# A written-out order for the first of six token blocks: six weight loads issued together, its last second products ahead of block two, one operation moved from POOL to DVE

## The chip, the cores and the metric

The kernel runs on one core of a Trainium2 chip. The metric is the device time of one execution in microseconds (us). The core has engines that each work through their own queue of instructions in order: PE (matrix products, its weight loads are shown as PEld), DVE (elementwise work on vectors, scans, 32x32 transposes), ACT (activations, casts, copies), POOL (elementwise work, masks) and SP, which here only issues transfers (DMA). An instruction that waits holds up everything behind it on its engine.

## The reference, cut to what matters

```
def _attn_ref(q, k, v, alpha):                 # (4, 8, 768, 48): batch, heads, steps, head size
    for t in range(S):
        state = alpha[:, :, t, :, None] * state + einsum('bhd,bhe->bhde', k[:, :, t], v[:, :, t])
        y[:, :, t] = einsum('bhd,bhde->bhe', q[:, :, t], state)

x = attn_out as (3072 tokens, 384)
h = x @ w_in;  g = h * sigmoid(1.702 h);  x = g @ w_out        # layer 1: 384 -> 2048 -> 384
h = x @ w_in2; g = h - tanh(h);           out = g @ w_out2     # layer 2, same sizes
```

A decayed linear attention over 768 steps is followed by two two-matrix layers on 3072 tokens. Everything is float32; the weights reach the chip as pairs of 32-bit words that the kernel turns into float32.

## The kernel before, in words

**Tokens.** The 3072 tokens are 24 chunks of 128 steps (g = 0 to 23), and 6 blocks of 512 tokens. A layer's block needs four chunks of attention output: block one the chunks 0 to 3, block two 4 to 7, block three 8 to 11. Each layer goes through its 6 blocks, each block through 16 weight tiles m (128 of the 2048 hidden columns each): 96 steps s for layer 1, then 96 for layer 2.

**One step.** `gemm1` (L455, 9 products of 128x128 by 128x512) makes the hidden values of tile m in one of two banks, `sig_1` (ACT, L472) the activation, `g_hi` (ACT, L475) a rounded copy ghi, `g_lo` (DVE, L478) the remainder glo, and `gemm2` (L461, 9 products, the third of each three reads glo) adds the tile's share to the block's three output banks. Every float32 operand is split in two parts (hi and lo), hence 9 products for 3 slices. From block two on, `gemm2` of step s comes three steps behind `gemm1` (LAG). After the 16th `gemm2` `evac` copies the three output banks to `xs` (ACT L516 twice, DVE L513 once) and stores them.

**Weights of layer 1.** In block one each tile is loaded (`w_given`, 768 KB on SP's queue) and converted: `w_bits` (DVE, L172 and L173), `w_join` (DVE, L185), `w_hi` (ACT, L204), `w_lo` (DVE, L208). `gemm1` of tile m needs w_hi in its first product and w_lo in its third.

**Attention of a chunk.** `a_load` (four transfers), two scans of the decay (`a_scan`: DVE L257 to L259, and L261), `a_scale` (L265, L266: k and q times the decay), the scores (`s_mm` L296 with copies and a mask on POOL L310 for the chunks below 8; `a_whole` L325, masked on DVE L328, from chunk 8 = FULL on), `a_turn` (DVE L335, transposes of k, from chunk 8 on), `a_out` (PE: L351 the carried state, L358 the values, and in `a_delta` L372 the state's growth, which reads the transposes), `a_state` (DVE L381, L382), then out and back: `a_evac` copies y out (ACT L416) and writes it to DRAM (four transfers, L421), `a_back` reads it back in the layer's layout (L431), and `x_hi` (ACT L438), `x_lo` (DVE L442) split it.

**Order.** Until block six of layer 1 every engine keeps the order of the code. For block one that is a table of words, one word one call: g `gemm1`, s `sig_1`, i `g_hi`, f `g_lo`, u `gemm2`, w `w_given`, b `w_bits`, j `w_join`, H `w_hi`, L `w_lo` of a tile; a `a_load`, p and q the two scans, k `a_scale`, t `a_state`, d `a_guard`, S `s_mm`, c and y its copies, O `a_out`, E `a_evac` and `a_back` with the load of the chunk three further on, X `x_hi`, x `x_lo` of a chunk. So g15 is `gemm1` of tile 15, X7 the cast of chunk 7. These names are used below; numbers from 16 on are steps of block two (g16 is its first `gemm1`). From block two on, `steady` places the parts d = 0, 1, 2 and 5 of chunk c of the next block at the steps STARTS[c] + d. Part 0 has for chunk 8 alone its own first transposes, then for every chunk the first scan of the next chunk and `a_whole`; part 1 the second transposes, the next chunk's second scan and scaling; part 2 the next chunk's first transposes and `a_out`.

Of the kernel before, what the change touches and what calls it, by code (L numbers as in the profile page):

```python
# [68 lines left out]
def linear_attention_mlps(ctx, tc, xq, xv, fa, fv, cst, w1, w2, out):  # L69
    nc = tc.nc  # L70
    V, A, G, P, SP = nc.vector, nc.scalar, nc.gpsimd, nc.tensor, nc.sync
# [74 lines left out]
    bank = [ps.tile([128, 512], F32, name=f"bank{i}") for i in range(8)]  # L146
# [30 lines left out]
    def w_check(l, m):  # L177
        t = wt[m % 2]
        tc.keep_in_program_order(V.tensor_scalar(out=t, in0=w_high(raw[2 if l == 1 else m % 3]), scalar1=0x3800, scalar2=0x7800,  # L179
                                                 op0=ALU.bitwise_xor, op1=ALU.bitwise_and))  # L180
        A.activation(out=t.bitcast(BF16), in_=t, func=AF.Square, accum_out=wsum[:, (l - 1) * MT + m :][:, :1])  # L181
# [48 lines left out]
    def dec3(g, n):  # L230
        return pairs(dec(g, n))[:, :: 1 if n else -1]


    def qq(g):
        return dec3(g, 2)

    def qkk(g):
        return dec3(g, 3)
# [22 lines left out]
            V.tensor_tensor_scan(out=dec(g, 1), data0=dec(g, 1), data1=seg, initial=0.0, op0=ALU.mult, op1=ALU.max)  # L261

    def a_scale(g):
        e = V if g < FULL else G
        e.tensor_tensor(out=qkk(g), in0=qkk(g), in1=dec3(g, 0)[:, :, :C], op=ALU.mult)  # L265
        e.tensor_tensor(out=qq(g)[:, :, :C], in0=qq(g)[:, :, :C], in1=dec3(g, 1)[:, :, 1:], op=ALU.mult)  # L266

# [62 lines left out]
    def a_turn(g, low):  # L330
        k = pairs(place_of(g)[3])
        for x in (0, 2) if low else (1, 3):
            d = kt8[g % 2][:, 4 * D * (x // 2) + 32 * (x % 2) :][:, : NP * D].rearrange("p (a d) -> p a d", a=NP)[:, :, :32]
            for y in range(4):
                V.transpose(out=d[32 * y : 32 * y + 32], in_=k[32 * x : 32 * x + 32, :, 32 * y : 32 * y + 32])  # L335
# [39 lines left out]
    def a_state(g):  # L375
        c = g % NCH
        if c < NCH - 1:
            dl = bank[7][:DP, : NP * D].rearrange("p (a e) -> p a e", a=NP)
            al = dec3(g + 1, 0)[:, :, C:].to_broadcast([DP, NP, D])
            if c:  # L380
                V.tensor_tensor(out=state, in0=dl, in1=state, op=ALU.add)  # L381
                V.tensor_tensor(out=state, in0=state, in1=al, op=ALU.mult)  # L382
            else:
                V.tensor_tensor(out=state, in0=dl, in1=al, op=ALU.mult)
# [125 lines left out]
    def evac(l, t0, n, acc, ks=range(KT)):  # L510
        for k in ks:
            if k == 1:
                V.tensor_scalar(out=xs[:, k, :n], in0=acc[k][:, :n], scalar1=1 / 1.702 if l == 1 else 1.0, scalar2=None,  # L513
                                op0=ALU.mult)
            else:
                A.activation(out=xs[:, k, :n], in_=acc[k][:, :n], func=AF.Copy, scale=1 / 1.702 if l == 1 else 1.0)  # L516
            if l == 2:
                SP.dma_start(out=out[k, :, t0 : t0 + n], in_=xs[:, k, :n])
        if l == 1:
            SP.dma_start(out=x1t[:, :, t0 : t0 + n].rearrange("k p t -> p k t"), in_=xs[:, :, :n])  # L520
# [11 lines left out]
    LAG = 3  # L532
# [28 lines left out]
    def prep(g, part):  # L561
        if g >= NG:
            return
        if part < 2:
            a_scan(g, part)
        if part == 2:
            a_scale(g)
        if part == 3:
            a_guard(g)
# [11 lines left out]
        if r == 2:  # L581
            a_out(g, b)

    STARTS = (0, 3, 7, 10)

    def steady(g, d):
        if d == 0:
            if g == FULL:
                a_turn(g, 0)
            prep(g + 1, 0)  # L590
            a_whole(g, 5)
        if d == 1:
            a_turn(g, 1)
            prep(g + 1, 1)
            prep(g + 1, 2)
            prep(g, 3)
        if d == 2:
            if g + 1 < NG:
                a_turn(g + 1, 0)
            a_out(g, 5)  # L600
            a_state(g)
            a_done(g)
        if d == 5:
            x_hi(g)
            x_lo(g)
# [99 lines left out]
    NS, NS1 = len(steps), len(L1) * MT  # L705
# [8 lines left out]
    def pads():  # L714
        for t in (*late, spare):
            SP.dma_start(out=t[3][DP:], in_=xq[0, : 128 - DP, : NP * C])
# [23 lines left out]
        "X": lambda g: x_hi(g, bank[5] if g == 3 else None),  # L740
        "x": lambda g: x_lo(g, bank[5] if g == 3 else None),
        "z": lambda _: pads(),
    }
    for word in """
        X1 L1 X3 d3 a6 w8 w9 w10 x1 b2 j2 x3 g0 H2 b3 g1
        s0 i0 L2 j3 g2 s1 f0 H3 b4 i1 u0 s2 f1 i2 L3 j4
        g3 f2 H4 b5 u1 s3 i3 L4 j5 u2 b6 H5 L5 g4 j6 f3
        H6 g5 p4 s4 i4 t3 u3 s5 q4 i5 L6 g6 f4 f5 b7 u4
        s6 i6 k4 u5 d4 b8 j8 S40 f6 H8 u6 b9 c40 y40 j7 S41
        L8 H7 c41 L7 g7 y41 p5 q5 O4 s7 i7 k5 E4 w11 w12 g8  # L750
        t4 d5 f7 j9 S50 s8 p6 H9 u7 c50 L9 y50 i8 q6 S51 g9
        c51 k6 y51 f8 O5 s9 b10 X4 i9 j10 E5 z0 w13 w14 u8 t5
        H10 f9 d6 p7 S60 u9 c60 L10 y60 q7 S61 b11 g10 c61 y61 j11
        b12 H11 O6 s10 i10 L11 X5 j12 g11 E6 w15 f10 H12 k7 u10 s11
        i11 t6 d7 x4 L12 S70 g12 b14 c70 y70 f11 S71 b13 s12 i12 u11
        c71 j13 y71 X6 f12 H13 O7 x6 L13 x5 E7 j14 g13 b15 H14 u12
        s13 L14 i13 j15 f13 H15 g14 p8 L15 u13 s14 i14 q8 X7 f14 k8
        g15 x7 t7 u14 s15
    """.split():
        part[word[0]](int(word[1:]))  # L760

    for s in range(MT, NS + LAG):
        if s:
            if s <= NS:
                l, j, m, i, t0, n, acc = place(s - 1)
                prev = s - 1, n
        if s < NS:
            l, j, m, i, t0, n, acc = place(s)
            h = HB[s % 2][:, :n]
            gemm1(i, m, h, n)  # L770
            if l == 2:
                tanh_near(s, h)
        if s <= NS:
            g_split(*prev)
        if s < NS and l == 1:
            sig_1(s, h, n)
        if s == NS:
            u_flag()
        if s < NS:
            if l == 1 and j + 1 < len(L1):  # L780
                t1, n1 = L1[j + 1]
                for c in range(4):
                    steady(t1 // C + c, m - STARTS[c])
            if l == 1 and 0 < j < len(L1) - 1 and m - 2 in STARTS:
                w_check(1, 4 * (j - 1) + STARTS.index(m - 2))
            if l == 1 and 0 < j < len(L1) - 1 and m in STARTS:
                w_load(1, 4 * (j - 1) + STARTS.index(m), 2)
            if l == 2 and 2 <= j < 4:
                if m % 2:
                    w_check(l, 8 * (j - 2) + m // 2)  # L790
                else:
                    tc.keep_in_program_order(w_load(l, 8 * (j - 2) + m // 2))
            if l == 1 and j == len(L1) - 1:
                if m == 0:
                    for q in range(3):
                        w_load(2, q)
                if m == 1:
                    a_flag()
                if m == 4:
                    x1_load(0)  # L800
                if m in (6, 7, 8):
                    x1_split(0, m - 6)
                if m > 0:
                    conv(2, m >= 4)
            if l == 2:
                if cv[2] < 2 * MT:
                    conv(2)
                if j == 4 and m == 3:
                    w_flag()
                if j + 1 < len(L2):  # L810
                    if m == 3:
                        x1_load(j + 1)
                    if m in (6, 7, 8):
                        x1_split(j + 1, m - 6)
        if s >= LAG:
            l, j, m, i, t0, n, acc = place(s - LAG)
            if s >= NS or s - LAG < 15:
                continue
            gemm2(m, s - LAG, acc, n)
            if m == MT - 1:  # L820
                evac(l, t0, n, acc)
        if s == (len(L1) - 1) * MT - 1:
            in_order(begin)


    l, j, m, i, t0, n, acc = place(NS - 1)
# [118 lines left out]
```

## Time and profile before

| | |
|---|---|
| time, median of 3 runs (range) | 925.53 us (924.96 to 928.22) |
| the profiled execution, its own time | 924.23 us |
| its span in the profile | 922.5 us |
| PE busy | 905.8 us (98%) |
| DVE / ACT / POOL busy | 668.6 (72%) / 449.5 (49%) / 98.5 us (11%) |
| mean granted TensorE clock | 0.998 |

The span runs from the first to the last instruction; 1.7 us of the execution's time lie around it. Times in rows are us from the span's start. Products are pipelined: one 128x512 product lasts some 0.4 us from start to end, but the next one starts 0.23 us after it, so a group is measured from its first start to the next group's first start. A row's brackets give the idle time of the engine just before it, and what ended that.

### The profile page before, as it was taken

To read this page: it belongs to the slowest core of one execution; us is meant where nothing else is said; L and a number is where in the kernel's file an instruction comes from. 1 tells how busy PE (TensorE), PEld (TensorE's weight loads), DVE (VectorE), ACT (ScalarE), POOL (GpSimd) and SP (SyncE) were. 2 spreads that over 40 slices of the span, in tenths; PEclk is the share of its full clock that TensorE was granted. 3 is DMA by queue.
4 is the path that set the end of the run, shared out by engine and by line. 5 is a ranking of instruction groups with operands and counts; after the bars stand their busy time and mean duration, and the time that the engine had idled before them with its cause. 6 is when DMAs were issued, how large, how long until landed. Compare 5 with 4: busy or idle time off the path is not lost.

```text
span 922.5 us, 13368 instructions
## 1 busy us (share of the span) xinstructions
PE 905.8 (98%) x4941; PEld 716.2 (78%) x4941; DVE 668.6 (72%) x1129; ACT 449.5 (49%) x907; POOL 98.5 (11%) x82
## 2 busy tenths in 40 slices
PE   9899899999999999999999999999999999999996
PEld 5777677777777778777888888888888888888885
DVE  8999787747657585776499966767777777666663
ACT  5646533434433433434445645554655665545552
POOL 6112021101111110111001002002001001000000
PEclk9999999999999999999999999999999999999999
DMA  8856734324341532536253300201323310000001
GB/s 223 282 182 185 212 93 160 93 89 133 115 147 47 169 99 82 180 102 223 85 176 131 137 1 2 101 1 31 140 92 114 137 68 1 35 1 1 34 1 39
DMA packets 56315, 95.61 MB, mean 104 GB/s; under 512 B 4864, under 2 KB 35712, under 8 KB 56240
## 3 DMA queue, kind: packets, MB, share of 16 engines
q1 hardware_dynamic: 55952, 94.27, 32.1%
q8 instruction: 40, 0.66, 0.3%
q10 hardware_dynamic: 288, 0.40, 0.1%
q14 instruction: 35, 0.29, 0.1%
HBM read 80.88 MB, written 13.76 MB: 103 GB/s over the span
## 4 chain that ended last, share of the span: by engine, by line
PE 86%; DVE 8%; DMA 3%; issue 1%; ACT 1%; SPq 0%; DVEq 0%; ACTq 0%
PE bank L461 41%; PE bank L455 39%; DMA given<-w 2%; PE bank L358 2%; PE bank L325 2%; PE bank L619 1%; DVE glo L478 1%; PE bank L351 1%; DVE cf L173 1%; DVE cf L335 1%; DVE w L208 1%; DVE arena L261 1%; PE bank L372 1%; DVE arena L258 1%; DVE cf L185 1%
## 5 line engine op out<-in xcount | busy, mean ns | idle before, releaser
L455 PE MATMUL bank<-xhi,w 128*128 128x512 f32 x1152 | 392.3, 395 | 2.4 <-DVE w L208 1.7
L461 PE MATMUL bank<-ghi,w 128*128 128x512 f32 x1152 | 366.4, 398 | 1.1 <-ACT xs L516 1.1
L455 PEld LDWEIGHTS bank<-xhi,w 128*128 128x128 f32 x1152 | 216.0, 188 | 55.6 <-DVE w L208 2.7
L461 PEld LDWEIGHTS bank<-ghi,w 128*128 128x128 f32 x1152 | 213.7, 188 | 53.9 <-issue 1.5
L478 DVE TENSOR_TENSOR glo<-gt,ghi 128x512 fp32r<-128x512 f32 x192 | 136.3, 710 | 148.0 <-ACT ghi L475 145.9
L461 PE MATMUL bank<-glo,w 128*128 128x512 f32 x576 | 228.2, 396 | 2.1 <-DVE glo L478 2.1
L455 PE MATMUL bank<-xlo,w 128*128 128x512 f32 x576 | 227.5, 396 | 2.1 <-DVE xlo L442 2.1
L475 ACT CAST ghi<-gt 128x512 fp32r<-128x512 f32 x192 | 118.9, 619 | 204.0 <-DVE gt L492 130.2
L461 PEld LDWEIGHTS bank<-glo,w 128*128 128x128 f32 x576 | 108.2, 188 | 29.3 <-DVE glo L478 2.9
L455 PEld LDWEIGHTS bank<-xlo,w 128*128 128x128 f32 x576 | 108.2, 188 | 28.5 <-DVE xlo L442 2.5
L472 ACT ACTIVATE gt<-bank 128x512 f32<-128x512 f32 x96 | 57.3, 597 | 116.2 <-PE bank L455 112.2
L490 DVE SCALAR_TENSOR_TENSOR arena<-arena,bank 128x512 f32<-128x512 f32 x96 | 65.8, 685 | 31.1 <-ACT arena L488 30.0
L492 DVE SCALAR_TENSOR_TENSOR gt<-arena 128x512 f32<-128x512 f32 x96 | 68.3, 712 | 10.5 <-DVE arena L491 0.9
L488 ACT ACTIVATE arena<-bank 128x512 f32<-128x512 f32 x96 | 57.3, 596 | 38.3 <-PE bank L455 37.8
L489 ACT ACTIVATE arena<-arena,cs 128x512 f32<-128x512 f32 x96 | 69.6, 726 | 3.0
L491 DVE SCALAR_TENSOR_TENSOR arena<-arena 128x512 f32<-128x512 f32 x96 | 67.9, 707 | 3.1
L529 POOL TENSOR_TENSOR xlo<-arena,xhi 128x512 fp32r<-128x512 f32 x18 | 28.0, 1582 | 339.9 <-ACT xhi L528 339.9
L335 DVE STREAM_TRANSPOSE cf<-arena 32x128 f32<-32x128 f32 x176 | 53.2, 302 | 2.5
L181 ACT ACTIVATE wtb<-wtb 128x768 bf16<-128x768 int16 x32 | 26.8, 837 | 47.7 <-DVE wtb L179 47.7
L442 DVE TENSOR_TENSOR xlo<-xlo,xhi 128x384 fp32r<-128x384 f32 x22 | 14.5, 660 | 26.0 <-ACT xhi L438 26.0
L265 POOL TENSOR_TENSOR arena<-arena 112x512 f32<-112x512 f32 x11 | 14.0, 1272 | 118.0 <-DVE seg L259 86.9
L310 POOL TENSOR_SCALAR_AFFINE_SELECT arena<-arena 128x512 f32<-128x512 f32 x16 | 18.4, 1161 | 70.7 <-ACT arena L308 62.8
(137 smaller groups left out, 646.2 us busy)
## 6 DMA issues: line engine op xcount, KB each, us to landing
raw<-w SPq DMA_DIRECT2D x48, 768.0 KB, 4.4
given<-w SPq DMA_DIRECT2D x16, 768.0 KB, 8.3
arena<-xq SPq DMA_DIRECT2D x32, 224.0 KB, 4.9
x1t<-xs SPq DMA_DIRECT2D x6, 768.0 KB, 5.3
arena<-x1t SPq DMA_DIRECT2D x6, 768.0 KB, 4.7
out<-xs SPq DMA_DIRECT2D x17, 256.0 KB, 2.3
xlo<-xt SPq DMA_DIRECT2D x22, 192.0 KB, 2.6
xt<-arena SPq DMA_DIRECT2D x76, 48.0 KB, 1.7
```

Of the source, the lines that this page charges most:

```text
L335: V.transpose(out=d[32 * y : 32 * y + 32], in_=k[32 * x : 32 * x + 32, :, 32 * y : 32 * y + 32])
L455: P.matmul(out=h, lhsT=w[m][:, ws], rhs=x[:, k, :n], start=c == 0, stop=c == 3 * KT - 1)
L461: P.matmul(out=acc[k][:, :n], lhsT=w[m][:, ws], rhs=x[s % 3][:, :n], start=m == 0 and c == 0, stop=m == MT - 1 and c == 2)
L472: A.activation(out=gb(s)[:, :n], in_=h, func=AF.Silu, scale=1.702)
L475: A.copy(ghi[s % 3][:, :n], gb(s)[:, :n])
L478: V.tensor_tensor(out=glo[s % 3][:, :n], in0=gb(s)[:, :n], in1=ghi[s % 3][:, :n].bitcast(F32), op=ALU.subtract)
L488: A.activation(out=u, in_=h, func=AF.Square, accum_out=usum[:, s - NS1 :][:, :1])
L489: A.activation(out=w, in_=u, func=AF.Square, bias=pbias)
L490: V.scalar_tensor_tensor(out=p, in0=u, scalar=P3, in1=h, op0=ALU.mult, op1=ALU.mult)
L491: V.scalar_tensor_tensor(out=p, in0=u, scalar=-PR, in1=p, op0=ALU.add, op1=ALU.mult)
L492: V.scalar_tensor_tensor(out=gb(s), in0=w, scalar=PD, in1=p, op0=ALU.add, op1=ALU.mult)
L529: G.tensor_tensor(out=xlo[i][:, k], in0=xr[:, k], in1=xhi[i][:, k].bitcast(F32), op=ALU.subtract)
```

## The change

Block one has a new table. Six loads (w8 to w13) are issued together where three were; the other two follow after the first chunk's E. `gemm2` of tile n comes right behind `gemm1` of tile n+1 in most places; the last one (u15) and the block's `evac` (new word e) stand at the table's end, ahead of block two, where u15 and `evac` came in block two's third step. In block two `steady` starts its first two chunks (8 and 9) at steps 1 and 4 where it was 0 and 3, and the weight checks go with them. `a_scale` of chunk 8 runs on DVE where it was POOL.

```
     def a_scale(g):
-        e = V if g < FULL else G
+        e = V if g <= FULL else G
...
-    STARTS = (0, 3, 7, 10)
+    def starts(j):
+        return (0, 3, 7, 10) if j > 1 else (1, 4, 7, 10)
...
+        "e": lambda _: evac(1, 0, NB, bank[:3]),
     }
     for word in """
-        X1 L1 X3 d3 a6 w8 w9 w10 x1 b2 j2 x3 g0 H2 b3 g1
...
-        s13 L14 i13 j15 f13 H15 g14 p8 L15 u13 s14 i14 q8 X7 f14 k8
-        g15 x7 t7 u14 s15
+        X1 L1 X3 x1 d3 a6 w8 w9 w10 w11 w12 w13 x3 g0 b2 g1
...
+        f13 g14 j15 E7 x5 H15 x6 u13 s14 L15 i14 f14 p8 q8 g15 u14
+        s15 i15 f15 t7 u15 X7 x7 k8 e0
     """.split():
...
-        if s <= NS:
+        if MT < s <= NS:
             g_split(*prev)
...
-                    steady(t1 // C + c, m - STARTS[c])
-            if l == 1 and 0 < j < len(L1) - 1 and m - 2 in STARTS:
-                w_check(1, 4 * (j - 1) + STARTS.index(m - 2))
-            if l == 1 and 0 < j < len(L1) - 1 and m in STARTS:
-                w_load(1, 4 * (j - 1) + STARTS.index(m), 2)
+                    steady(t1 // C + c, m - starts(j)[c])
+            if l == 1 and 0 < j < len(L1) - 1 and m - 2 in starts(j):
+                w_check(1, 4 * (j - 1) + starts(j).index(m - 2))
+            if l == 1 and 0 < j < len(L1) - 1 and m in starts(j):
+                w_load(1, 4 * (j - 1) + starts(j).index(m), 2)
...
-            if s >= NS or s - LAG < 15:
+            if s >= NS or s - LAG < MT:
                 continue
```

**Place one.** DVE at the start of block one, before (w_456 is converted tile 1, given_65 the loaded tile 2, bank_110 holds chunk 3's values in the layer's layout):

```order
L208 TENSOR_TENSOR w_456<-cf_83,w_456 128x768
L442 TENSOR_TENSOR xlo_87<-xlo_87,xhi_85 128x3x128
L172 TENSOR_SCALAR cf_84<-given_65 128x768
L173 SCALAR_TENSOR_TENSOR cf_84<-given_65,cf_84 128x768
L185 SCALAR_TENSOR_TENSOR cf_84<-given_65,cf_84 128x768
L442 TENSOR_TENSOR xlo_87<-bank_110,xhi_85 128x3x128
```

The same place of the changed kernel:

```order
L208 TENSOR_TENSOR w_456<-cf_83,w_456 128x768
L442 TENSOR_TENSOR xlo_87<-xlo_87,xhi_85 128x3x128
L442 TENSOR_TENSOR xlo_87<-bank_110,xhi_85 128x3x128
L172 TENSOR_SCALAR cf_84<-given_65 128x768
L173 SCALAR_TENSOR_TENSOR cf_84<-given_65,cf_84 128x768
L185 SCALAR_TENSOR_TENSOR cf_84<-given_65,cf_84 128x768
L478 TENSOR_TENSOR glo_93<-gt,ghi_90 128x512
```

x3, which g0's seventh product reads, stood behind b2 and j2 and now stands ahead of them.

**Place two.** SP's queue from w8 (given_71) on, before; xt is the chunk's output in DRAM, xlo its read-back, arena the inputs of a later chunk:

```order
L162 DMA given_71<-w 128x1536
L162 DMA given_72<-w 128x1536
L162 DMA given_73<-w 128x1536
L421 DMA xt<-arena 48x2x128 x4
L431 DMA xlo_88<-xt 128x3x128
L251 DMA arena<-xq 112x516
L251 DMA arena<-xq 112x512
L251 DMA arena<-xq 112x4x128
L251 DMA arena<-xv 128x384
L162 DMA given_74<-w 128x1536
L162 DMA given_75<-w 128x1536
L421 DMA xt<-wtb 48x2x128 x4
```

And in the changed kernel:

```order
L162 DMA given_71<-w 128x1536
L162 DMA given_72<-w 128x1536
L162 DMA given_73<-w 128x1536
L162 DMA given_74<-w 128x1536
L162 DMA given_75<-w 128x1536
L162 DMA given_76<-w 128x1536
L421 DMA xt<-arena 48x2x128 x4
L431 DMA xlo_88<-xt 128x3x128
```

The loads of tiles 11 to 13 moved ahead of chunk 4's round trip (E4); those of 14 and 15 follow E4 in the changed kernel, where 13 and 14 followed E5 and 15 followed E6.

**Place three.** DVE at the border of blocks one and two, before, from f15 (glo_93) to the second transposes of chunk 8:

```order
L478 TENSOR_TENSOR glo_93<-gt,ghi_90 128x512
L335 STREAM_TRANSPOSE cf_82<-arena 32x4x32 x8
L257 MEMSET seg 112x4
L258 SCALAR_TENSOR_TENSOR raw<-raw,seg 112x516
L259 RECIPROCAL seg<-raw 112x4
L328 TENSOR_TENSOR arena<-bank_110,cs 128x512
L328 TENSOR_TENSOR arena<-bank_111,cs 128x512
L478 TENSOR_TENSOR glo_94<-gt,ghi_91 128x512
L335 STREAM_TRANSPOSE cf_82<-arena 32x4x32 x8
```

In the changed kernel, from chunk 8's scaling on:

```order
L265 TENSOR_TENSOR arena<-arena 112x512
L266 TENSOR_TENSOR arena<-arena 112x4x128
L513 TENSOR_SCALAR xs<-bank_106 128x512
L478 TENSOR_TENSOR glo_94<-gt,ghi_91 128x512
L335 STREAM_TRANSPOSE cf_82<-arena 32x4x32 x8
L257 MEMSET seg 112x4
L258 SCALAR_TENSOR_TENSOR raw<-raw,seg 112x516
L259 RECIPROCAL seg<-raw 112x4
L328 TENSOR_TENSOR arena<-bank_110,cs 128x512
L328 TENSOR_TENSOR arena<-bank_111,cs 128x512
L478 TENSOR_TENSOR glo_95<-gt,ghi_92 128x512
L335 STREAM_TRANSPOSE cf_82<-arena 32x4x32 x8
```

The transposes of chunk 8 now stand one glo further back: the first set behind f16 (glo_94), the second behind f17. On PE, chunk 8's `a_whole` now follows g17 and its `a_out` follows g19, where they followed g16 and g18; u15 stood behind that `a_out`, and u16 stands behind it now.

## Rows read from the trace of the kernel before

**Rows 1.** Stretches: length; busy PE, PEld, DVE, ACT, POOL (x instructions); clock; DMA share; GB/s.
```profile
32.04:120.25 88.21, 82.20 (x504) 61.91 (x504) 80.42 (x112) 47.43 (x100) 13.64 (x10) 1.00 0.69 214
...
136.69:915.00 778.31, 778.31 (x3996) 623.08 (x3996) 543.85 (x930) 375.33 (x733) 65.74 (x46) 1.00 0.27 88
```

**Rows 2.** Timeline of PE: start, us, instructions, and in brackets idle before.
```profile
35.78 0.96 PE L455 MATMUL bank<-xlo,w 128*128 128x512 f32 x3 [2.10 <-DVE xlo L442]
...
101.43 0.50 PE L461 MATMUL bank<-glo,w 128*128 128x512 f32 x1 [2.06 <-DVE glo L478]
...
111.96 0.73 PE L455 MATMUL bank<-xhi,w 128*128 128x512 f32 x2 [1.68 <-DVE w L208]
...
117.87 0.63 PE L461 MATMUL bank<-ghi,w 128*128 128x512 f32 x2
...
136.69 0.73 PE L461 MATMUL bank<-ghi,w 128*128 128x512 f32 x2 [1.06 <-ACT xs L516]
```

**Rows 3.** Timeline of DVE: the two long waits for loaded weight tiles.
```profile
98.78 0.56 DVE L172 TENSOR_SCALAR xs<-given 128x768 int32<-128x768 int32 x1 [3.72 <-DMA given<-w]
...
109.48 0.56 DVE L172 TENSOR_SCALAR cf<-given 128x768 int32<-128x768 int32 x1 [2.38 <-DMA given<-w]
```

**Rows 4.** The chain that ended last: one group of nine products, start and us.
```profile
141.13 2.09 PE bank L461 x9
```

**Rows 5.** Timeline of ACT: the cast i15, whose gemm1 ended where rows 2 have 117.87.
```profile
118.70 0.62 ACT L475 CAST ghi<-gt 128x512 fp32r<-128x512 f32 x1
```

**Rows 6.** Timeline of DVE: what the words L, j, f and b take.
```profile
37.10 0.95 DVE L208 TENSOR_TENSOR w<-cf,w 128x768 fp32r<-128x768 f32 x1
37.98 0.95 DVE L185 SCALAR_TENSOR_TENSOR xs<-given,xs 128x768 int32<-128x768 int32 x1
38.84 0.68 DVE L478 TENSOR_TENSOR glo<-gt,ghi 128x512 fp32r<-128x512 f32 x1
39.45 0.55 DVE L172 TENSOR_SCALAR xs<-given 128x768 int32<-128x768 int32 x1
40.03 0.96 DVE L173 SCALAR_TENSOR_TENSOR xs<-given,xs 128x768 int32<-128x768 int32 x1
```

**Rows 7.** Timeline of DVE: from f15 to chunk 8's second transposes.
```profile
120.50 0.69 DVE L478 TENSOR_TENSOR glo<-gt,ghi 128x512 fp32r<-128x512 f32 x1
...
123.79 0.06 DVE L257 MEMSET seg<- 112x4 f32 x1
...
125.25 1.26 DVE L328 TENSOR_TENSOR arena<-bank,cs 128x512 f32<-128x512 f32 x2
...
127.03 2.52 DVE L335 STREAM_TRANSPOSE cf<-arena 32x128 f32<-32x128 f32 x8
```

**Rows 8.** Timeline of PE: a_whole and a_out of chunk 8, and chunk 9's L372.
```profile
122.44 1.16 PE L325 MATMUL bank<-arena 48*128 48x128 f32 x16
...
127.91 0.66 PE L351 MATMUL bank<-arena,state 48*48 48x128 f32 x16
...
129.41 0.75 PE L372 MATMUL bank<-arena,cf 128*48 128x48 f32 x16
...
146.74 0.53 PE L372 MATMUL bank<-raw,cf 128*48 128x48 f32 x16
```

**Rows 9.** A stretch of block one, columns as in rows 1.
```profile
32.00:59.00 27.00, 24.86 (x106) 19.91 (x107) 26.14 (x39) 13.59 (x22) 0.00 (x0) 1.00 1.03 325
```

**Rows 10.** Timeline of SP's issues: the round trips of chunks 6 and 8.
```profile
92.41 2.69 SPq L421 DMA_DIRECT2D xt<-arena  x4
99.59 0.40 SPq L431 DMA_DIRECT2D xlo<-xt  x1
...
129.81 1.78 SPq L421 DMA_DIRECT2D xt<-arena  x4
...
133.10 0.40 SPq L431 DMA_DIRECT2D xlo<-xt  x1
```

**Rows 11.** Timeline of ACT: chunk 6's cast after that read-back.
```profile
102.19 0.51 ACT L438 CAST xhi<-xlo 128x384 fp32r<-128x384 f32 x1 [2.17 <-DMA xlo<-xt]
```

More of the change, by code (lines that the diff above doesn't have):

```diff
@@ L742, in linear_attention_mlps @@
         "z": lambda _: pads(),
+        "e": lambda _: evac(1, 0, NB, bank[:3]),
     }
     for word in """
-        X1 L1 X3 d3 a6 w8 w9 w10 x1 b2 j2 x3 g0 H2 b3 g1
[L746 to L756, printed above, removed]
-        s13 L14 i13 j15 f13 H15 g14 p8 L15 u13 s14 i14 q8 X7 f14 k8
-        g15 x7 t7 u14 s15
+        X1 L1 X3 x1 d3 a6 w8 w9 w10 w11 w12 w13 x3 g0 b2 g1
+        s0 j2 i0 H2 f0 b3 u0 s1 i1 L2 g2 j3 f1 H3 b4 u1
+        s2 i2 L3 f2 g3 j4 p4 H4 u2 s3 i3 L4 f3 g4 b5 j5
+        u3 s4 b6 H5 i4 L5 g5 f4 j6 b7 H6 u4 s5 i5 L6 g6
+        j7 f5 H7 q4 u5 s6 i6 k4 S40 t3 d4 L7 g7 f6 c40 p5
+        y40 S41 s7 q5 i7 u6 c41 k5 y41 O4 b8 j8 E4 w14 w15 S50
+        t4 H8 f7 d5 u7 L8 c50 b9 y50 S51 j9 g8 c51 b10 H9 y51
+        j10 O5 s8 i8 L9 H10 f8 X4 g9 L10 E5 z0 x4 p6 g10 s9
+        i9 q6 u8 s10 f9 i10 k6 u9 f10 t5 d6 b11 S60 X5 j11 u10
+        c60 b12 y60 H11 S61 L11 g11 c61 j12 y61 p7 H12 O6 s11 L12 i11
+        f11 E6 q7 g12 k7 u11 s12 b13 i12 f12 S70 j13 u12 c70 b14 y70
+        H13 L13 S71 g13 j14 c71 y71 t6 X6 H14 b15 O7 s13 i13 L14 d7
+        f13 g14 j15 E7 x5 H15 x6 u13 s14 L15 i14 f14 p8 q8 g15 u14
+        s15 i15 f15 t7 u15 X7 x7 k8 e0
     """.split():
```

## The prediction

> **What bounds the kernel now.** I read the stretches first. From 136.69 to 915 PE is busy in all 778.31 us [rows 1]: nothing there waits, and nothing there can give back or swallow what happens earlier. So whatever PE gains or loses before 136.69 reaches the end one to one. In block one and its border PE does wait: from 32.04, where g0 begins, to 120.25, where g16 begins, it is busy 82.20 of 88.21 us [rows 1], 6.01 idle. The timeline of PE names most of it: 2.10 us in g0 for x3, 2.06 for a glo, 1.68 for a w_lo [rows 2], the missing 0.17 in scraps. In block two it waits once more, 1.06 us at u16, for the block's evac on ACT [rows 2]. The timeline of DVE tells why a glo and a w_lo were late: DVE stood 3.72 and 2.38 us in front of b14 and b15, whose weight tiles had not landed [rows 3]. A seventh wait hides inside a group: L372 of chunk 8 took 0.75 us where that of chunk 9 took 0.53 [rows 8], because chunk 8's second transposes ended only at 127.03 + 2.52 = 129.55 [rows 7]: 0.22 us.
>
> **What goes.** The three sums 6.01 + 1.06 + 0.22 = 7.29 us are all that the change can win; PE's work stays the same (16 gemm1 and gemm2 in block one, every group 2.09 [rows 4], so 0.23 a product). Piece by piece:
> - x3 now stands ahead of b2 and j2. It can begin when g0 does; as a subtract it is no longer than an f, 0.68 [rows 6], and g0 reads it at its seventh product, 1.4 us after its start. The 2.10 go whole.
> - The tiles 14 and 15 are now issued behind E4. O4 ends after 15 groups (g0 to g7, u0 to u6) of 2.1 us and some 4 us of attention, near 67.5, while b14 and b15 stood at 98.78 and 109.48 [rows 3]. The loads have over 20 us, and the 2.06 and 1.68 go.
> - evac is issued behind u15, and u16 comes only after g16 to g19, over 8 us later. The 1.06 go.
> - The 0.22 go too, but only because something larger takes their place.
>
> **What comes, first: chunk 8's a_out.** The transposes for L372 used to begin right behind f15. Now the first set stands behind f16, so it waits for g16, s16 and i16. An i ends 118.70 + 0.62 = 119.32, when its gemm1's slot ended at 117.87 [rows 2, 5]: f16 can begin 1.5 us after g16's slot. From the start of the f ahead of the first transposes to the end of the second ones DVE needs 129.55 - 120.50 = 9.05 us without a pause [rows 7], so they end 10.55 after g16. PE has g17, L325, g18, g19 and the first part of a_out to do: 3 x 2.1 + 1.16 + 1.50 (129.41 - 127.91) [rows 4, 8] = 9.0. L372 waits 1.5 us. Behind it on PE stand u16 and everything else, so the 1.5 are paid. The lower bound is 0 only if DVE could begin before f16, which its queue excludes; each us by which f16 comes later than 1.5 adds one. I take 1.5. Chunk 9 has no such wait: its first transposes were done a part earlier.
>
> **Second: gemm2 close behind gemm1.** An f ends 1.5 + 0.68 = 2.18 us after its gemm1's slot; u(n) now mostly follows g(n+1) and reads glo at its third product, 2.1 + 0.47 = 2.57 after. That leaves 0.39 us for whatever DVE has in front of the f. I added up DVE's queue by the durations of [rows 6, 7] (start to start L 0.88, j 0.86, f 0.61, b 1.5, p 1.46). The first tight place is g5: f0 begins at 32.04 + 2.1 + 1.5 = 35.64; f0 to f3, b3 to b6, L2 to L5, j3 to j5 and p4 make 16.0, so L5 is done near 51.6; g5 needs it after nine groups and two products, at 51.4. Some 0.2 us. In the same way S50 waits about 0.15 for E4's copies and g11 about 0.4 for L11, where the masks on POOL and DVE's queue meet. That is 0.8; I take 1.0. As bounds: DVE is busy 80.42 us [rows 1], with f15 81.1, and PE's work is 82.20 + 2.1 = 84.3. If DVE pauses only where it did apart from the two load waits (88.21 - 80.42 - 3.72 - 2.38 = 1.7) it is done at 82.8 and PE sets the end: 0 us. If it pauses 7.8 as before, it needs 88.9 and the block ends 4.6 later.
>
> **At nothing.** k8 on DVE is two products of the kind of f, up to 1.4 us, behind x7, which alone g16 needs; with L513 (another 0.7) it lies in the 3.6 us in which DVE waits for i16 anyway. Without that cover it costs 1.4. x7 itself: u15 no longer stands behind g16, so chunk 7's round trip has only g14, u13, g15, u14 and u15, 10.5 us, between O7 and g16. ACT starts E7's copies about 1.5 late (s13, i13, d7), and X7 and x7 take 1.0, so some 8.0 remain from the first write's issue to the landing. Chunk 6's took 102.19 - 92.41 = 9.8 with tiles in the queue ahead of it [rows 10, 11]; its read-back went out 7.2 after the first write, chunk 8's on a quiet queue 3.3 [rows 10], so a quiet trip takes 5.9. At that time no tiles are left to load: 0 us, up to 1.8 if it is as slow as chunk 6's. The parts of chunks 8 and 9 a step later end well ahead of block three.
>
> The six loads: the DMA engines are full up to 59 at 325 GB/s [rows 9]. Three more tiles of 0.79 MB take 7.3 us, so the queue empties near 66.3, and E4's writes come near 68. They cost nothing, by 2 us. The Trainium skill (DMA: Bandwidth & Descriptors, section Queues, rings and completion order) speaks against this step: each DMA engine takes a queue's descriptors in ring order, so a small round trip issued behind big loads waits for all of them. By that rule the sum would lose what X4 comes late if the queue were still full at 68. The trace agrees with the rule: 7.2 against 3.3 us above.
>
> **The sum.** 7.29 - 1.5 - 1.0 = 4.8 us. Against the profiled execution, 924.23, that is 919.4; this execution lies 0.14% below the median of the runs shown (925.53), and the median moved by the same share is 920.7, or 0.52% faster. A measurement of this kernel tells about 0.5%, 4.6 us, from no change, so the forecast stands on that line.
>
> **The rivals.**
> - Clean: f16 earlier or the transposes shorter than added up, no new waits in block one. For it: PE's work and DVE's both fit. Against it: the queue order, which puts f16 ahead of the transposes. Gain 5.8 to 7.3, or 918.2 to 919.7 for the median.
> - DVE becomes the bound of block one: it is 96% of PE's work there, its masks on POOL and its loads come as they come. Gain 7.29 - 1.5 minus 2.3 to 4.6, so 1.2 to 3.5: 922.0 to 924.3. A late X7 gives about the same (4.8 - 1.8 = 3.0, 922.5).
> - The loads get in the way of E4 (the rule above) or the waits for tiles only move: the read-back up to 7.3 late, X4 and all behind it on ACT with it, less 2 us in hand. Gain about 0: 925.5.
> - Slower: the f's. If f comes late for each of the 16 tiles, PE loses at every u. By 0.36 us each beyond the margin (0.75 of delay in all) the 5.8 left after a_out are gone; by 0.65 each (10.4 in all) the kernel is 0.5% slower, near 930. For it: DVE has no slack between 32 and 59, 26.14 busy of 27.00 [rows 9]. Against it: by the sums above DVE is at f ahead of need at most tiles.
>
> **How the numbers follow.** Forecast (gain 3.5 to 5.8, 919.7 to 922.0) 0.46; clean 0.18; DVE or X7 0.25; about nothing 0.05; slower 0.06. Faster by over 0.5% has the clean case and somewhat over half of the forecast's: 0.45. Slower takes 0.05, and the rest, 0.50, lies within 0.5%, though most of it below the old median. The range leaves out the lower half of the clean case and the last two: 918.2 to 924.0.
>
> **What would show it.** Right: no PE wait in g0; no DVE wait for given near b14 and b15; no wait of u16 for xs; one PE wait of about 1.5 us at L372 of chunk 8, released by DVE's transposes; g16 near 117 instead of 120.25, and u16 about 5 us earlier than 136.69; PE busy throughout from there. Wrong: waits of PE for glo or w before many u's (DVE bound), a wait of ACT for xlo at X4, X5 or X7, or a PE wait after block two.

## The result, and the profile after

The changed kernel takes **918.31 us** (median of 6 executions, 917.51 to 919.37) where the kernel before took 925.30 beside it (6 executions, 923.94 to 928.22): ratio **0.9918, 95% interval 0.9900 to 0.9936**, so 0.8% faster. Its profiled execution took 918.35 us, span 916.5 (before 924.23 and 922.5): 6.0 us less. The forecast was 920.7 and 4.8 us less; the time lies at the low edge of the range, and beyond the 0.5% line on which the forecast stood.

The timeline of PE after, from g0 to u16, all the rows behind g0's start that have a bracket, with g16's start and the product group ahead of the last wait:

```profile
51.99 0.72 PE L455 MATMUL bank<-xhi,w 128*128 128x512 f32 x2 [0.21 <-DVE w L208]
...
77.31 0.73 PE L455 MATMUL bank<-xhi,w 128*128 128x512 f32 x2 [0.29 <-DVE w L208]
...
116.35 0.39 PE L455 MATMUL bank<-xhi,w 128*128 128x512 f32 x1
...
126.09 0.66 PE L351 MATMUL bank<-arena,state 48*48 48x128 f32 x16
...
127.76 0.29 PE L372 MATMUL bank<-arena,cf 128*48 128x48 f32 x2
129.04 0.56 PE L372 MATMUL bank<-arena,cf 128*48 128x48 f32 x14 [0.99 <-DVE cf L335]
129.53 0.73 PE L461 MATMUL bank<-ghi,w 128*128 128x512 f32 x2
```

All four waits of [rows 2] are gone. In block one stand 0.21 at g5 and 0.29 at g9, both for a w_lo; at the border 0.99 for chunk 8's transposes. Some more waits of block one have no bracket: they show only in how far apart the starts lie, and are priced below. The stretches that answer to [rows 1]:

```profile
32.16:116.35 84.19, 83.69 (x513) 64.01 (x513) 80.29 (x115) 47.59 (x101) 7.70 (x8) 1.00 0.68 213
129.53:909.00 779.47, 779.47 (x4014) 623.91 (x4012) 546.17 (x942) 374.55 (x732) 68.04 (x47) 1.00 0.27 88
```

PE is idle 0.50 of 84.19 us in block one, and not at all from u16 on. DVE from f16 to the second transposes, where [rows 7] stood:

```profile
119.92 0.69 DVE L478 TENSOR_TENSOR glo<-gt,ghi 128x512 fp32r<-128x512 f32 x1 [2.63 <-ACT ghi L475]
120.64 2.52 DVE L335 STREAM_TRANSPOSE cf<-arena 32x128 f32<-32x128 f32 x8
...
125.87 0.68 DVE L478 TENSOR_TENSOR glo<-gt,ghi 128x512 fp32r<-128x512 f32 x1
126.47 2.52 DVE L335 STREAM_TRANSPOSE cf<-arena 32x128 f32<-32x128 f32 x8
```

They end at 126.47 + 2.52 = 128.99, and L372 goes on at 129.04. No DVE row has a wait for given any more ([rows 3] had 3.72 and 2.38). SP's issues of two round trips, chunks 4 and 5:

```profile
68.18 1.77 SPq L421 DMA_DIRECT2D xt<-arena  x4
71.33 0.40 SPq L431 DMA_DIRECT2D xlo<-xt  x1
...
73.78 0.90 SPq L162 DMA_DIRECT2D given<-w  x2
77.97 1.79 SPq L421 DMA_DIRECT2D xt<-wtb  x4
84.37 0.40 SPq L431 DMA_DIRECT2D xlo<-xt  x1
```

E4's writes come at 68.18 (the prediction had 68) and its read-back goes out 3.15 us later, the quiet 3.3 of [rows 10]: the six loads are out of the way. E5's, behind the two loads issued at 73.78, goes out 6.40 later. The Trainium skill (DMA: Bandwidth & Descriptors, section Queues, rings and completion order) states that each DMA engine takes a queue's descriptors in ring order; 3.15 against 6.40 agrees with it. On ACT it costs X5 a wait of 1.95, one of the prediction's signs of being wrong, and the wait is handed on, from ACT to DVE to PE:

```profile
86.89 0.51 ACT L438 CAST xhi<-xlo 128x384 fp32r<-128x384 f32 x1 [1.95 <-DMA xlo<-xt]
...
88.10 0.87 ACT L204 CAST w<-cf 128x768 fp32r<-128x768 f32 x1
...
89.00 0.96 DVE L208 TENSOR_TENSOR w<-cf,w 128x768 fp32r<-128x768 f32 x1 [0.73 <-ACT w L204]
...
90.01 0.73 PE L455 MATMUL bank<-xhi,w 128*128 128x512 f32 x2
```

X5 holds up H11 (88.10), for which L11 on DVE waits 0.73, and g11's third product starts 0.05 behind L11's end. It has no bracket, but g11 takes 0.26 longer than such a group does elsewhere. So the late read-back cost 0.26 us, not nothing.

**Where the 6.0 us come from.** Before, g0 to g16 took 88.21 us without u15 [rows 1]; after, 84.19 with it. For the same work that is 88.21 + 2.09 - 84.19 = 6.1 us. From g16 to the end the two differ by nothing: 922.5 - 120.25 - 2.09 = 800.16 against 916.5 - 116.35 = 800.15, so the new wait at L372 took back what u16's wait and the old 0.22 gave. g0 started 0.1 later. Of the 6.1, idle time is 6.01 - 0.50 = 5.5; the other 0.6 is **busy** time, 82.20 + 2.09 against 83.69.

That part was not in the prediction. Two rows of before show it, g14's start and that of u13 behind it, with the wait of 1.68 [rows 2] between:

```profile
109.65 0.39 PE L455 MATMUL bank<-xhi,w 128*128 128x512 f32 x1
...
113.70 0.62 PE L461 MATMUL bank<-ghi,w 128*128 128x512 f32 x2
```

4.05 us, where a group takes 2.09: the wait cost 1.96. In front of a wait, 0.17 (a product's 0.40 less the 0.23 after which the next may start) counts as busy though nothing new starts; and the first product behind a wait takes about 0.1 more. So a wait of less than 0.17 shows no idle time and still costs. Rows of small waits, before g7's 0.16 and u14, which starts 0.41 behind the product ahead of it and has no bracket, and after S50, whose eight products take 1.04 to the next start where others take 0.80:

```profile
66.56 0.73 PE L455 MATMUL bank<-xhi,w 128*128 128x512 f32 x2 [0.16 <-DVE seg L257]
...
118.51 0.50 PE L461 MATMUL bank<-glo,w 128*128 128x512 f32 x1
```

```profile
68.24 1.11 PE L296 MATMUL bank<-arena 48*128 48x176 f32 x8
```

Measured in this way for every group between g0 and g16 (2.09 without a wait, 0.1 more behind attention's products and 0.1 more ahead of them), the waits cost:

| gone: place | bracket | cost | new: place | bracket | cost |
|---|---|---|---|---|---|
| g0, x3 | 2.10 | 2.34 | g5, w_lo | 0.21 | 0.46 |
| u11, glo | 2.06 | 2.32 | g9, w_lo | 0.29 | 0.56 |
| g14, w_lo | 1.68 | 1.96 | g11, w_lo | none | 0.26 |
| g7 | 0.16 | 0.42 | S50 | none | 0.24 |
| g11, g13, u14 | none | 0.55 | g2, g13 | none | 0.14 |
| together | 6.0 | 7.6 | together | 0.5 | 1.7 |

In the new order S50 follows O4 directly, which saves one change from attention's products to those of 512 columns and back, 0.2 us. 7.6 - 1.7 + 0.2 = 6.1, the whole gain of block one.

### The profile page after: what moved, and what is told of

It reads as the page before. It is cut to its first block, busy times and chain, and to the rows that moved or that the text cites. A ratio compares the mean times of both kernels' runs of the same rounds, so it can differ in the third digit from the quotient of the medians.

```text
span 916.5 us, 13370 instructions
## 1 busy us (share of the span) xinstructions
PE 904.0 (99%) x4941; PEld 716.2 (78%) x4941; DVE 666.0 (73%) x1131; ACT 449.2 (49%) x907; POOL 93.5 (10%) x80
## 4 chain that ended last, share of the span: by engine, by line
PE 92%; DVE 5%; ACT 1%; issue 1%; DMA 0%; POOL 0%; ACTq 0%; DVEq 0%; POOLq 0%
PE bank L461 43%; PE bank L455 42%; PE bank L358 2%; PE bank L325 2%; PE bank L296 1%; PE bank L351 1%; PE bank L372 1%; DVE glo L478 1%; DVE w L208 1%; DVE xs L173 1%; DVE cf L335 0%; PE bank L402 0%; DVE cf L185 0%; DMA cs<-cst 0%; DVE xs L185 0%
## 5 line engine op out<-in xcount | busy, mean ns | idle before, releaser
L335 DVE STREAM_TRANSPOSE cf<-raw 32x128 f32<-32x128 f32 x80 | 24.2, 303 | 1.1
L310 POOL TENSOR_SCALAR_AFFINE_SELECT arena<-arena 128x512 f32<-128x512 f32 x16 | 16.3, 1028 | 75.2 <-ACT arena L308 40.2
```

## Experiments

Medians of the same chip's runs of the kernel before are 924.6 to 926.1. All ratios are to that kernel:

| run | median us | ratio, 95% interval | span |
|---|---|---|---|
| e1_x3 | 925.03 | 1.0001, 0.9992 to 1.0011 | 924.3 |
| e2_loads | 919.90 | 0.9947, 0.9930 to 0.9963 | 918.6 |
| e3_evac | 924.45 | 0.9994, 0.9981 to 1.0007 | 923.4 |
| e8_three | 919.44 | 0.9948, 0.9928 to 0.9969 | 916.7 |
| e7_late | 924.65 | 1.0000, 0.9987 to 1.0013 | 922.9 |
| e5_starts | 917.23 | 0.9920, 0.9899 to 0.9941 | 915.8 |
| e6_pool | 918.50 | 0.9932, 0.9914 to 0.9951 | 916.8 |
| e4_turn | 916.77 | 0.9920, 0.9899 to 0.9942 | 915.1 |
| after_again | 918.66 | 0.9927, 0.9911 to 0.9943 | 916.4 |
| e4_again | 916.90 | 0.9903, 0.9887 to 0.9918 | 915.9 |
| e9_best | 917.93 | 0.9931, 0.9915 to 0.9947 | 916.2 |
| e11_best | 918.40 | 0.9923, 0.9907 to 0.9938 | 919.1 |
| e10_fill | 918.57 | 0.9922, 0.9901 to 0.9942 | 917.2 |
| e12_fill | 924.12 | 0.9990, 0.9977 to 1.0003 | 923.5 |

### One part alone on the kernel before

**x3 ahead of b2 and j2:**

```
-  ... x1 b2 j2 x3 g0 H2 ...
+  ... x1 x3 b2 j2 g0 H2 ...
```

> The kernel before with one word moved: x3 ahead of b2 and j2. Theory A (a wait of PE is worth the idle time in its brackets): the 2.10 us go, span 922.5 - 2.1 = 920.4. Theory B (a wait also costs the pipeline's emptying and refilling, some 0.25 us each, which the profile counts as busy): 2.35 go, span near 920.1, and PE's busy time falls by 0.25. Rival: the wait only moves to the next late word, span unchanged.

Measured: no change. The wait in g0 is gone, and g1 starts 2.24 us earlier than before (34.34 against 36.58). But by g7 nothing is left of that: its third product starts at 66.59 here and at 66.56 before (above). DVE sets the pace between; it has no idle time to speak of from 36 us on, as the row of this run from 40 to 60 us shows (19.49 us busy of 20), and it reaches the same place at the same time:

```profile
66.59 0.74 PE L455 MATMUL bank<-xhi,w 128*128 128x512 f32 x2 [0.26 <-DVE seg L257]
```

```profile
40.00:60.00 20.00, 19.87 (x84) 15.46 (x84) 19.49 (x29) 9.36 (x15) 0.00 (x0) 1.00 1.03 309
```

So in the old order of words x3's wait only moves into several smaller ones. Behind that, two waits of PE are longer than the 2.06 and 1.68 of [rows 2]:

```profile
101.77 0.50 PE L461 MATMUL bank<-glo,w 128*128 128x512 f32 x1 [2.16 <-DVE glo L478]
...
113.41 0.72 PE L455 MATMUL bank<-xhi,w 128*128 128x512 f32 x2 [2.78 <-DVE w L208]
```

and so are DVE's two in front of them [rows 3]:

```profile
99.12 0.56 DVE L172 TENSOR_SCALAR xs<-given 128x768 int32<-128x768 int32 x1 [3.83 <-DMA given<-w]
...
110.93 0.56 DVE L172 TENSOR_SCALAR cf<-given 128x768 int32<-128x768 int32 x1 [3.48 <-DMA given<-w]
```

No run shows that the last of these is an effect of the edit. Tile 15 was taken up 8.4 us after its load was issued (102.49), in the profiled execution of before after 7.4 (102.04 to 109.48) and in that of e12, which keeps the order of before, after 8.7: this time differs by over 1 us between executions.

**The six loads together, the last two behind E4:**

```
-  ... w8 w9 w10 x1 ...   E4 w11 w12 ...   E5 z0 w13 w14 ...   E6 w15 ...
+  ... w8 w9 w10 w11 w12 w13 x1 ...   E4 w14 w15 ...   E5 z0 ...   E6 ...
```

> The kernel before with the loads alone moved: w8 to w13 together, w14 and w15 behind E4. A: the 2.06 and 1.68 go, span 918.8; B: 4.2 go, span near 918.3. Rival (the six loads stand in E4's way): X4 waits for its read-back and most of the gain is lost, 921 to 922.5.

Measured: 0.5% of the 0.8%. Of PE's waits only 1.92 in g0 and 0.44 at u16 are left; by the brackets alone 4.7 us went, which would give 917.8. That the span of 918.6 lies between the two theories is luck: something else took time back, and the windows of this run show it (below, with e10).

**u15 and evac ahead of block two:**

```
-  ... u14 s15
+  ... u14 s15 i15 f15 u15 e0
```

> The kernel before with u15 and evac alone ahead of block two (chunk 8 at step 0 and on POOL as before). A: the 1.06 go, span 921.4; B: 1.3 go, 921.2. Rival: L513 now stands in front of chunk 8's first transposes on DVE and L372 waits longer, then 921.5 to 922.5.

Measured: no change within 0.2%, an interval that a gain of 1.06 us (0.11%) fits as well as none. The trace settles it better: from g16 to the end it takes 923.4 - 124.39 = 799.0 us, 1.1 less than the 800.16 of before without u15, so u16's wait was won. This execution lost more than that ahead of the border, in a wait of 2.84 us for g14's w_lo at 112.71 where there were 1.68, with a clock of 0.50 behind it. The moved words stand behind that place on every engine, so the edit did not make that wait longer; tile 15 was taken up 8.6 us after its issue here.

**These three edits at once, the old order otherwise:**

> The three edits of e1, e2 and e3 on the old table, without the new order, the later steps and the move to DVE. A: 2.10 + 3.74 + 1.06 = 6.9 go, span 915.6; B: 8.15, span 914.4, that is below the changed kernel's 916.5, since neither L372's 1.5 nor the two short waits of the new order come in. Rival: with the waits gone DVE becomes the bound in the old order and glo or w are late elsewhere, span 916 to 919; then the new order was needed.

Measured: 0.5%. The span of 916.7 is 1.1 above the 915.6 that the sum of the brackets gave, in the rival's range. No bracket is left after 70 us, but four small ones have come into block one:

```profile
37.06 0.50 PE L455 MATMUL bank<-xhi,w 128*128 128x512 f32 x1 [0.43 <-ACT gt L472]
38.03 0.73 PE L455 MATMUL bank<-xhi,w 128*128 128x512 f32 x2 [0.25 <-DVE w L208]
...
65.62 0.50 PE L455 MATMUL bank<-xhi,w 128*128 128x512 f32 x1 [0.59 <-ACT w L204]
66.61 0.72 PE L455 MATMUL bank<-xhi,w 128*128 128x512 f32 x2 [0.26 <-DVE seg L257]
```

The last comes at the same 66.6 as in e1 and before: again DVE's pace. The span is nearly the changed kernel's 916.5, but not for the same reason. The new order brings g16 to 116.35 where it stands at 117.90 here (u15 ahead of it in both), 1.55 earlier; from g16 to the end the changed kernel then needs 800.15 us and this one 798.8, because of L372's wait. So the new order wins back in block one what DVE's pace takes there, and in the changed kernel that and L372's wait nearly cancel. How much of it is x3's is not shown: the changed kernel with x3 at its old place was not run. The medians can't show it: the intervals of 0.9948 here and of the changed kernel's 0.9918 and 0.9927 overlap.

### One part of the changed kernel undone

**The loads back at their old places, the new order kept:**

```
-  ... w8 w9 w10 w11 w12 w13 x3 ...   E4 w14 w15 ...   E5 z0 x4 ...   E6 q7 ...
+  ... w8 w9 w10 x3 ...   E4 w11 w12 ...   E5 z0 w13 w14 x4 ...   E6 w15 q7 ...
```

> The changed kernel with the loads issued where they were before (w11 and w12 behind E4, w13 and w14 behind E5, w15 behind E6). If the loads carry their 4 us in the new order too: 920 or so. From the rows of the changed kernel: b15 stands at 103.0 and w15 would land near 105 to 106.5, 2 to 3.5 late, g15 has 1.5 in hand and b13, b14 are about in time: PE loses 0.5 to 2.5, span 917 to 919.

Measured: the whole gain is gone, more than either figure expected (span 922.9). One wait for the last tile takes it, on DVE and behind it on PE:

```profile
107.69 0.56 DVE L172 TENSOR_SCALAR cf<-given 128x768 int32<-128x768 int32 x1 [4.82 <-DMA given<-w]
```

```profile
110.17 1.22 PE L455 MATMUL bank<-xhi,w 128*128 128x512 f32 x2 [3.86 <-DVE w L208]
```

Two products that take 0.73 elsewhere take 1.22 here; the clock (third from the end) shows why, 0.67 in the window in which PE stood idle and 0.50 in the next:

```profile
108.00:110.00 2.00, 0.00 (x0) 0.00 (x0) 1.97 (x3) 0.00 (x0) 0.00 (x0) 0.67 0.20 50
110.00:112.00 2.00, 1.83 (x4) 1.49 (x5) 2.00 (x5) 0.38 (x1) 0.00 (x0) 0.50 0.68 186
```

With e2 this run settles that the early loads carry the gain: with them alone most of it is there, without them none.

**Block two's chunks at their old steps; chunk 8's scaling back on POOL:**

```
-        return (0, 3, 7, 10) if j > 1 else (1, 4, 7, 10)
+        return (0, 3, 7, 10) if j > 1 else (0, 3, 7, 10)
```

> The changed kernel with chunks 8 and 9 back at steps 0 and 3 of block two. The chain of DVE to L372 then starts when L513 ends, at 117.3, without f16 in front, and ends 8.3 later, 125.6; PE is there at 125.4: L372 waits 0.2 and 1.2 us go, span 915.3. If the step later was needed for something else (x7, the scores' bank), span 916.5 or more.

```
-        e = V if g <= FULL else G
+        e = V if g < FULL else G
```

> The changed kernel with chunk 8's scaling back on POOL, the one part that the prediction put on DVE at nothing. Theory, that DVE has room there and POOL too: median within 0.6 of the changed kernel's 918.3 to 918.7, chunk 8's L325 and L372 where they were. Rival, that POOL is slower at it and chunk 8's products come late: a wait of PE at chunk 8's L325, and 0.6 to 2 us more.

Measured: the first has no bracket at L372, only the 0.2 that were expected, hidden in a group of 0.76 where e4 below takes 0.53:

```profile
125.63 0.76 PE L372 MATMUL bank<-arena,cf 128*48 128x48 f32 x16
```

From g16 to the end it takes 799.3 us against the changed kernel's 800.15, so in the traces the later start costs 0.8 us; the ratio of 0.9920 is level with the changed kernel's 0.9918 and 0.9927 (it ran on another chip than those two). The later start is no part of the gain. The second, 918.50, lies between the changed kernel's two medians and has its waits of 0.18, 0.26 and 0.99: the scaling is worth nothing on either engine, as the prediction had it.

### The new wait at L372

**Chunk 8's first transposes at the table's end, ahead of f16:**

```
-            if g == FULL:
-                a_turn(g, 0)
...
+        "T": lambda g: a_turn(g, 0),
...
-        s15 i15 f15 t7 u15 X7 x7 k8 e0
+        s15 i15 f15 t7 u15 X7 x7 k8 e0 T8
```

> The changed kernel with chunk 8's first transposes issued at the end of the table, ahead of f16 instead of behind it. They take 2.52 us and DVE stands idle for 2.63 there, so the chain to L372 is 2.5 shorter: L372 waits for nothing and the 1.49 us of a_out go, span 916.5 - 1.5 = 915.0. Rival (L372's wait hides another behind it, a_state or u16): less than 0.5 gained.

and once more beside the changed kernel on one chip:

> The changed kernel with chunk 8's first transposes ahead of f16, a second time. If its wait for chunk 8's evacuation costs what the bracket and its restart say (0.99 and about 0.25), it stands 1.2 to 1.6 below the changed kernel on this chip; if the one run on another chip misled, 0 to 0.6.

> The changed kernel itself, once more, beside its successors on one chip. Every theory: a median of 917.5 to 919.4, span near 916.5, the same two waits of 0.2 and 0.3 in block one and the one of 1.0 for chunk 8's evacuation; if its clock stays near 0.998 and that of the kernel before scatters lower, the theory that part of the gain is the clock's is borne out once more.

Measured: 916.77, then 916.90 against 918.66 (916.07 to 917.59 against 918.13 to 920.09, no overlap), 1.8 us, a little more than the 1.2 to 1.6 expected. The timeline of PE in e4_turn, from the same group on:

```profile
125.76 0.66 PE L351 MATMUL bank<-arena,state 48*48 48x128 f32 x16
...
127.25 0.53 PE L372 MATMUL bank<-arena,cf 128*48 128x48 f32 x16
127.71 0.73 PE L461 MATMUL bank<-ghi,w 128*128 128x512 f32 x2
```

From L351 to u16 this takes 1.95 us; in the changed kernel it took 129.53 - 126.09 = 3.44. The wait cost 1.49, by the very queue order that the prediction named: f16 ahead of the transposes. This is the fastest version found.

**Block one's DVE words moved, on top of it** (first e9, then e11):

```
-  ... j4 p4 H4 ...   s4 b6 H5 i4 L5 g5 f4 j6 ...   L9 H10 f8 X4 g9 L10 ...
+  ... j4 H4 ...   H5 s4 b6 L5 i4 g5 f4 p4 j6 ...   L9 H10 L10 f8 X4 g9 ...
```

> The changed kernel with the transposes of e4, p4 moved from ahead of H4 to behind f4, H5 and L5 ahead of s4's and b6's ends (H5 s4 b6 L5), and L10 ahead of f8: the three waits of PE left in the profile, 0.21 at g5, 0.29 at g10 and L372's, are aimed at. A: 1.5 + 0.5 go, span 914.5; B: another 0.5, span 914.0. Rival: each move makes another word late (L5 then waits for H5 on DVE), 914.5 to 915.5.

```
-  ... j4 p4 H4 ...   s4 b6 H5 i4 ...   f5 H7 q4 ...   j10 O5 s8 i8 L9 H10 ...
+  ... j4 H4 ...   H5 s4 b6 i4 ...   f5 H7 p4 q4 ...   L9 O5 s8 i8 j10 H10 ...
```

> The changed kernel with the transposes ahead of f16, and in block one p4 later, H5 ahead of s4, L9 ahead of j10. Theory, that VectorE is late for g5 and g9 by the one word in front of it: both waits (0.20 and 0.31) go, with their restarts, span 914.0 to 914.6. Rival, that block one's VectorE has no slack and another word comes late: 915.1 or more, with a new wait of 0.2 to 0.8.

Measured: neither beats e4. In e9 (beside e4_turn on one chip) g6 waits 0.73 at 57.30 for its w_lo; in e11 (beside e4_again) S40 is late by 1.44 at 62.12, for the scaling behind p4 and q4. Behind that wait the clock falls to 0.50, too (64 to 66 us). DVE's queue in block one has no slack to hand out.

### The clock behind a long wait

**Eight added products where e2 waits in g0** (into a bank that holds nothing needed; the rest is e2):

```
+            if fill and c == 6:
...
+                for _ in range(8):
+                    P.matmul(out=bank[4], lhsT=wf, rhs=..., start=True, stop=True)
```

> The kernel before with the loads as in e2, and eight added products of 128 columns by 512 into a bank that nothing reads yet, between the sixth and the seventh product of the first group, where TensorE waits 1.92 us for x3 in e2. They are added work and leave nothing out. Theory, that the clock falls because TensorE stood idle before: the wait becomes 0 to 0.3, the stretch from 36 to 40 us shows a clock of 1.00, and the span comes out 1.3 to 1.9 below e2's, 916.7 to 917.3. Rival, that the clock falls from another cause and only happens to follow the wait: the clock is still near 0.5 there, and the span stays within 0.4 of 918.6.

Windows of e2, columns as in rows 1, the clock the third from the end:

```profile
34.00:36.00 2.00, 0.16 (x1) 0.16 (x2) 1.97 (x4) 0.65 (x1) 0.00 (x0) 1.00 1.00 403
36.00:38.00 2.00, 2.00 (x7) 1.59 (x8) 1.97 (x3) 1.25 (x3) 0.00 (x0) 0.67 1.07 242
38.00:40.00 2.00, 2.00 (x6) 1.55 (x5) 2.00 (x4) 0.15 (x1) 0.00 (x0) 0.50 1.07 280
```

The same windows of e10:

```profile
34.00:36.00 2.00, 1.56 (x8) 0.48 (x5) 1.97 (x4) 0.40 (x1) 0.00 (x0) 1.00 1.01 404
36.00:38.00 2.00, 1.91 (x8) 1.60 (x9) 1.97 (x4) 1.26 (x3) 0.00 (x0) 1.00 1.05 239
38.00:40.00 2.00, 2.00 (x10) 1.61 (x10) 2.00 (x4) 1.22 (x3) 0.00 (x0) 1.00 1.16 249
```

Behind e2's wait the granted clock falls to 0.5, 1.2 GHz, and six products pass in 2 us where ten do at 1.00. With the wait filled by work that nobody needs (0.54 of it is left) the clock stays up, and the span is 1.4 us shorter, as the first theory had it. The Trainium skill (TensorE: Matmul & The Clock Gate, section Part 1: The HAM clock gate) states that an idle TensorE's clock is at half; these rows agree on the level, 0.50, and on idleness as the cause.

**The kernel before with products added at its three waits:**

```
+        if first and m == 14:
+            fill(h, 6)
...
+            if first and m == 0 and c == 6:
+                fill(bank[4], 8)
...
+                if first and m == 11 and k == 0 and c == 2:
+                    fill(bank[4], 8)
```

`fill(b, count)` issues `count` such products into the bank b.

> The kernel before with added products, and nothing left out: eight of 128 columns by 512 between the sixth and the seventh product of g0, eight ahead of the first product of u11 that reads glo, six ahead of g14's first, into banks that hold nothing needed. They stand where TensorE waits 2.10, 2.06 and 1.68 us and take 0.23 us each, less than the waits. Theory, that the kernel before loses time twice in these waits, once by standing idle and in part of its executions again by a granted clock of 0.5 behind them: the work that counts still starts at the same times, the span of an execution without such a stretch stays at 922.5, but all executions now have a mean clock of 0.997 or more (before: 0.994 to 0.999), and the median falls by 0.5 to 1.7 against before. Rival, that the executions of before differ by when their loads land, and the clock only follows: the clock stays at 0.994 to 0.996 in most executions, median within 0.4 of before.

Measured (the added products are work on top, of 0.23 us each): all 12 executions have a mean clock of 0.997 to 0.999. Of the 17 of the kernel before on that chip, 6 have 0.993 to 0.995 and a median of 926.8, and the other 11, at 0.996 to 0.998, one of 924.4. The median with the fills, 924.12, lies 0.8 us below before. That the clock falls because of the waits is borne out; that it costs 0.8 of the median is not shown, the interval holds "no difference" too. The scatter that is left, 922.98 to 926.23 at a full clock, is not the clock's. In the profiled one of these executions the loads came late:

```profile
99.11 0.56 DVE L172 TENSOR_SCALAR xs<-given 128x768 int32<-128x768 int32 x1 [4.26 <-DMA given<-w]
...
111.04 0.56 DVE L172 TENSOR_SCALAR cf<-given 128x768 int32<-128x768 int32 x1 [3.61 <-DMA given<-w]
```

against 3.72 and 2.38 [rows 3], at a span of 923.5, with no load moved. On this chip the changed kernel with its scaling on POOL took 918.50: against e12 5.6 us less, against the kernel before 6.4.

## Why the prediction was too cautious

Its mechanism held. PE was full behind the border, so the gain passed to the end; x3, the glo, the w_lo and the evac waits went; the loads ended before E4's writes; the scaling and X7 cost nothing. L372 was forecast at 1.5 us and cost 1.49, and the steps of that sum came true: DVE's transposes ended 10.55 us behind g16's slot, as worked out. g16 came at 116.35 (near 117 forecast).

**The step that failed is "The three sums ... are all that the change can win; PE's work stays the same".** It took the idle brackets for the cost of a wait. The waits that went from block one were put in at 6.0 and cost 7.6, 1.6 more, and the 1.6 stand in the busy time. Three smaller terms were off as well:
- The new waits in block one were added up to 0.8 and taken at 1.0; they cost 1.7, by the same error. The places were mostly right: g5 (priced 0.2, cost 0.46), S50 (0.15, 0.24) and g11 (0.4, 0.26, but by way of X5, H11 and L11 instead of the masks on POOL). g9's 0.56 was not foreseen.
- The new order saves one change between attention and the layer's products, 0.2, for which no term stood; and the border was forecast to lose 0.2 net and lost nothing.
- The forecast for the median moved the profiled execution's gain by one share. Before, the median of 925.30 is 1.1 above the profiled execution; after, 918.31 is level with its. So the medians differ by 1.0 more than the profiled pair. Executions of before with a mean clock of 0.993 to 0.995 are 2.4 slower than the others (e12's chip), and no term stood for them; whether that is the whole 1.0 is open, since e12 kept the clock up and moved its median by 0.8, which is not clear of noise.

Together: 4.8 + 1.6 - 0.7 (new waits) + 0.2 (change saved) + 0.2 (border) - 0.1 (g0 later) = 6.0 for the profiled pair, and 7.0 for the medians. Most of it points one way, which the chances did not: on a forecast at the line they gave "within 0.5%" 0.50 and "faster" 0.45.

Of the rivals, **clean** had the right time (918.2 to 919.7) for a reason that did not happen: f16 still stands ahead of the transposes, L372 waits, and block one has new waits. **DVE as the bound** did not come in the new order, PE being busy 83.69 of 84.19 us; in the old one it did (e1, e8), and e9 and e11 show how close it is: one word too early for another tile makes a wait of 0.7 to 1.4. **Loads in the way** was right about the queue (E5 at 6.40 us, though not E4); its price was 0.26, not the whole gain. **Slower** did not come.

## What to carry to other kernels

Price a wait from start to start of the products around it, not by its idle bracket: in this kernel that was about 0.25 us more for each wait, and some waits had no bracket at all. Look at the clock of several executions, since TensorE may lose once more behind a wait (in e11 behind 1.44 us). Before an early wait is taken out, look which engine sets the pace behind it: with DVE full, x3's 2.1 us were gone again 30 us later (e1, e8). When one trace has scatter of its own, as tile 15's landing has, compare it stretch by stretch with the other: that showed evac's 1.1 us, which the times could not. And when a step is pushed behind an operation in a queue, as the transposes behind f16, add up the queue to the next need: here that sum was right within 0.1, and undoing the one move gave 1.5 us in the traces and 1.8 in the medians.

## What was not expected of the hardware

The granted clock fell to 0.5 behind waits of PE of 1.44 us (e11), 1.92 (e2), 2.78 (e1), 2.84 (e3) and 3.86 (e7). A window behind the shortest of them, in e11, and one in e1:

```profile
64.00:66.00 2.00, 2.00 (x6) 1.52 (x5) 1.89 (x5) 0.73 (x4) 1.34 (x1) 0.50 0.93 381
```

```profile
114.00:116.00 2.00, 2.00 (x6) 1.51 (x5) 1.96 (x4) 0.84 (x1) 0.00 (x0) 0.52 0.91 264
```

Yet the profiled execution of the kernel before kept 1.00 behind 2.10, 2.06 and 1.68, and e12 behind 1.62. So the length of the wait alone does not decide it, and the mean clocks of before, 0.993 to 0.999, differ between executions of one program; what decides it is not settled here.
